# Three small moves in a retention and mixture-of-experts kernel: one subtraction to GpSimd, one copy to ScalarE, and the order of the loads

## The chip, the core and the metric

The kernel runs on one core of a Trainium2 chip. A core has five engines that run beside each other and wait for each other through semaphores: TensorE (PE in the profile, its weight loads PEld) multiplies matrices, VectorE (DVE) and ScalarE (ACT) do elementwise work, GpSimd (POOL) does elementwise work on on-chip memory and indirect transfers, and SyncE (SP) hands transfers to the core's DMA engines. Each engine works through its instructions in a fixed order. The metric is the device time of one execution in microseconds, lower is better.

## What is computed

The reference has two stages. The first is a retention layer for 8 sequences of 576 positions with 8 heads of width 64; the second sends each of the 4608 resulting rows to one of eight experts:

```
scores = q @ k^T / sqrt(64)                    # per head
ret    = scores * gamma[h] ** (i - j)  for i >= j, else 0
x      = ret @ v                               # 4608 rows of 512
expert = argmax(normalised x . normalised expert_emb / tau)
gate   = softmax(...)[expert]
out    = gate * (relu(x @ w1[expert]) @ w2[expert])    # w1 512x1024, w2 1024x512
```

All tensors are float32.

## The kernel before

**Retention.** A loop over the eight sequences (called batches, b = 0 to 7) holds a loop over four pairs of heads (p = 0 to 3). A sequence is cut into four chunks of 128 positions and a rest of 64. Within a chunk the masked scores are made directly: `emit_A` multiplies keys and queries on TensorE into a PSUM bank of the pool "a", and VectorE multiplies them by the triangle (line 623) into a buffer named raw. `emit_At` and line 719 do the same for the rest of 64 (tile pt). What earlier chunks contribute goes through a running state T: `emit_U(b)` multiplies keys and scaled values of each chunk into two PSUM banks of the pool "m" (rows named m<-vt,kt), and VectorE copies the first chunk's product into the state (line 651) and adds the others, one after the other (three instructions of line 653). `emit_QT` multiplies queries by the state and `emit_O` the scores by the values, both into a bank of the pool "o", of which there are two; `emit_Ot` does both for the rest of 64. `emit_X` (lines 705, 707 and 708) scales a finished "o" bank into the tile xT or xC on VectorE, and so frees the bank. The state of batch b+1 is made at the end of batch b.

**Loads.** `load_qk(b, p)` brings 576 KB of queries and keys of a pair of heads, `load_k(b)` 1024 KB of keys by chunk and `load_v(b)` 1152 KB of values, all for the next batch and all through SP (lines 481, 489 and 498). There are seven buffers for the first, two for each of the others. `scale_v(b)` multiplies the values by powers of gamma on GpSimd, in four instructions of 128x512 and one of 128x256 (lines 591 and 595); `emit_U(b)` needs them.

**Routing beside it.** Tasks of the batch before are set between the products: `route_tile` turns a 128-row tile of x by TensorE, ScalarE copies it from a PSUM bank to a buffer y (line 768), SP stores it to HBM (line 770, xd<-y), and ScalarE squares it (line 772). `route_head`, `route_rank`, `route_onehot` and `route_table` choose the experts on VectorE with small instructions (lines 207 to 341; line 209 subtracts the maximum, both of its inputs in on-chip memory).

**The first expert's weight.** In batches 2 to 5, at p = 1, one of the four tasks of `wsplit_tasks(0)` is started: SP loads a quarter of w1[0] (line 179, raw<-w, 512 KB), ScalarE rounds it to the high part (line 182), and VectorE subtracts that from the weight to get the low part (line 183). The experts' products use a high and a low part of weights and rows. Weights of n = 1 to 15 are split in the expert stage by the same function.

**Experts.** From about 180 us on TensorE runs the expert products (lines 120 and 971).

**What sets the order.** The program's text gives each instruction a priority by its place. A planner then goes through simulated time and hands each engine the first instruction by priority that it takes to be ready then. A load that the text has late can so come ahead of others when its buffer is free early (keys do so), and a store whose data is late falls behind. The resulting order of each engine is fixed, and on the chip an instruction that waits holds back all behind it on its engine.

Of the kernel before, what the change touches and what calls it, by code (L numbers as in the profile page):

```python
# [20 lines left out]
NP = H // 2  # L21
# [76 lines left out]
def retention_moe(ctx: ExitStack, tc: tile.TileContext, qk, kv, embT, tau, w1, w2, cst, out):  # L98
    nc = tc.nc
# [19 lines left out]
    def mm(*args, **kw):  # L119
        pe[:] = [nc.tensor.matmul(*args, **kw)]  # L120
        return pe[0]
# [5 lines left out]
    def behind():  # L127

        return ExitStack()
# [6 lines left out]
    def cc(name):  # L136
        o, w = _C[name]
        return cs[:, o : o + w]
# [27 lines left out]
    def wsplit_tasks(n):  # L166

        e, second = divmod(n, 2)
        src = (w2 if second else w1)[e]

        def step(c):
            raw = rawp.tile([P, RW], F32, name="raw")[:, :1024]
            if second:
                nc.sync.dma_start(
                    out=raw.rearrange("p (c n) -> p c n", c=2),
                    in_=src[c * 256 : (c + 1) * 256, :].rearrange("(c p) n -> p c n", p=P),
                )
            else:
                nc.sync.dma_start(out=raw, in_=src[c * P : (c + 1) * P, :])
            sl = wslot[n % 3]  # L180
            hi = sl[:, 0, c * 1024 : (c + 1) * 1024]
            nc.scalar.copy(hi, raw)  # L182
            nc.vector.tensor_tensor(  # L183
                out=sl[:, 1, c * 1024 : (c + 1) * 1024], in0=raw, in1=hi.bitcast(F32), op=ALU.subtract
            )

        return [lambda c=c: step(c) for c in range(4)]
# [283 lines left out]
    with ExitStack() as att:  # L471
# [7 lines left out]
        def load_qk(b, p):  # L479
            t = qkp.tile([P, 2, S], F32, name="qkt")  # L480
            nc.sync.dma_start(out=t, in_=qk[b, p])
            qkt[b, p] = t
# [4 lines left out]
        def load_k(b):  # L487
            t = a1.tile([P, KW], F32, name="kt", bufs=2)
            nc.sync.dma_start(out=t, in_=kv[b, :, :KW])
            kt[b] = t  # L490

        def load_v(b, split=False):
            t = a2.tile([P, KW + NP * D], F32, name="vt")
            if split:
                for lo, hi in [(c * DM, (c + 1) * DM) for c in range(NCH)] + [(KW, KW + NP * D)]:
                    nc.sync.dma_start(out=t[:, lo:hi], in_=kv[b, :, KW + lo : KW + hi])
            else:
                nc.sync.dma_start(out=t, in_=kv[b, :, KW:])
            vt_[b] = t
# [77 lines left out]
        def kview(b):  # L577
            return kt[b].rearrange("p (c n) -> p c n", c=NCH)

        def vview(b):  # L580
            return vt_[b][:, :KW].rearrange("p (c h d) -> p c h d", c=NCH, h=H)

        def vtview(b):
            return vt_[b][:, KW:].rearrange("p (r d) -> p r d", r=NP)

        def scale_v(b):
            eng = nc.vector if b == 0 else nc.gpsimd
            g = cc("gneg").rearrange("p (c h) -> p c h", c=NCH)
            v = vview(b)
            for c in range(NCH):  # L590
                eng.tensor_tensor(  # L591
                    out=v[:, c], in0=v[:, c], in1=g[:, c].unsqueeze(2).broadcast_to([P, H, D]), op=ALU.mult
                )
            vt = vtview(b)
            eng.tensor_tensor(
                out=vt, in0=vt, in1=cc("gnegt").unsqueeze(2).broadcast_to([P, NP, D]), op=ALU.mult
            )

        def turn_k(p):

            ps = psm.tile([P, 512], F32, name="m")
            for c in range(NCH):
                tr(ps[:, c * P : (c + 1) * P], qkt[0, p][:, 1, c * P : (c + 1) * P], ident)
            nc.scalar.copy(kview(0)[:, :, p * P : (p + 1) * P], ps.rearrange("p (c n) -> p c n", c=NCH))
# [3 lines left out]
        def emit_A(b, p):  # L608
            t = qkt[b, p]
            ps = [psa.tile([P, 512], F32, name="a") for _ in range(2)]  # L610
            for c in range(NCH):
                for h in range(2):
                    hs = slice(h * D, (h + 1) * D)
                    mm(
                        ps[h][:, c * P : (c + 1) * P],
                        t[hs, 1, c * P : (c + 1) * P],
                        t[hs, 0, c * P : (c + 1) * P],
                        start=True,
                        stop=True,
                    )  # L620
            pm = rawp.tile([P, RW], F32, name="raw")[:, :1024].rearrange("p (h c n) -> p h c n", h=2, c=NCH)
            for h in range(2):
                nc.vector.tensor_tensor(  # L623
                    out=pm[:, h],
                    in0=ps[h].rearrange("p (c n) -> p c n", c=NCH),
                    in1=tri.unsqueeze(1).broadcast_to([P, NCH, P]),
                    op=ALU.mult,
                )
            Pm[b, p] = pm

        def emit_U(b):
            k, v, T = kview(b), vview(b), Tst[b % 2]
            for c2 in range(NCH // 2):
                ps = psm.tile([P, 512], F32, name="m")
                u = ps.rearrange("p (c r d) -> p c r d", c=2, r=NP)
                for ci in range(2):
                    c = 2 * c2 + ci
                    for p in range(NP):
                        for h in range(2):
                            hd = 2 * p + h  # L640
                            mm(
                                u[h * D : (h + 1) * D, ci, p, :],
                                k[:, c, hd * D : (hd + 1) * D],
                                v[:, c, hd, :],
                                start=True,
                                stop=True,
                            )
                for ci in range(2):
                    c = 2 * c2 + ci
                    if c == 0:  # L650
                        nc.vector.tensor_copy(T[:, 0], u[:, 0])
                    else:
                        nc.vector.tensor_tensor(out=T[:, c], in0=u[:, ci], in1=T[:, c - 1], op=ALU.add)

# [178 lines left out]
        for b in range(B):  # L833
            for p in range(NP):
                if b + 1 < B:
                    load_qk(b + 1, p)
                    if p == 0:
                        load_v(b + 1)
                        load_k(b + 1)
                        scale_v(b + 1)  # L840
                if p + 1 < NP:
                    if b > 0 or p == 2:
                        with behind() if b > 0 else ExitStack():
                            emit_A(b, p + 1)
                else:
                    with behind():
                        if b + 1 < B:
                            emit_A(b + 1, 0)
                    with behind():
                        emit_At(b)  # L850
                    with behind():
                        if b + 1 < B:
                            emit_U(b + 1)
                if b == 0 and p == 0:
                    for r in range(NP):
                        turn_k(r)
                    emit_U(0)
                for _ in range(POPS[p] if b == B - 1 else 0):
                    if tasks:
                        tasks.pop(0)()  # L860
                if b == 0 and p < 2:
                    emit_O(b, p, True)
                    if p == 1:
                        emit_QT(b, 0, False)
                        emit_X(b, 0)
                        emit_X(b, 1)
                else:
                    if p % 2 == 0:
                        with behind():
                            emit_QT(b, p, True)  # L870
                    with behind() if b > 0 else ExitStack():
                        emit_O(b, p, False)
                    emit_X(b, p)
                if p == NP - 1:
                    with behind():
                        emit_Ot(b)
                if b < B - 1 and p in SLOTS and tasks:
                    with behind():
                        for task in tasks.pop(0):
                            task()  # L880
                if 1 < b < 6 and p == 1 and wq:
                    wq.pop(0)()
            if b < B - 1:
                tasks += route_tasks(b)
        b = B - 1
# [14 lines left out]
    with ExitStack() as moe:  # L900
# [88 lines left out]
        for e in range(NE):  # L989
            if e + 1 < NE:  # L990
                wq += wsplit_tasks(2 * e + 2)
            if e == 0:
                b = B - 1
# [241 lines left out]
```

## Time and profile before

| | |
|---|---|
| median of 3 runs | 612.83 us (610.84 to 613.12) |
| the profiled execution's own time | 612.28 us |
| its span, first to last instruction | 610.5 us |
| granted TensorE clock | 0.997 |
| PE busy, share of the span | 589.7 us, 97% |
| DVE, ACT, POOL busy | 330.7, 210.7, 176.8 us |
| bytes moved by DMA | 109.77 MB |

A row of a timeline reads: start in us from the span's start, length in us, engine, line, operation, output tile and input tiles, shape, how many instructions are merged in the row, and in brackets how long the engine was idle before it and what ended that. "SPq" is SyncE handing in a transfer. A row of grouped lines has the count, then busy time in us and mean ns of one, then the idle time before them with its causes. A row of waits has the total in us, the number of waits and the longest.

### The profile page before, as it was taken

How to read it: one execution, taken by the hardware profiler on the slowest of the kernel's cores; microseconds unless marked ns; L12 is line 12 of the kernel's file. 1: busy time of each engine (PE TensorE's matmuls, PEld its weight loads, DVE VectorE, ACT ScalarE, POOL GpSimd, SP SyncE). 2: the span in 40 equal slices, each digit the busy share in tenths (PEclk: the TensorE clock that was granted, in tenths of full speed). 3: DMA queues.
4: the chain of work that ended last, by engine and by line, in shares of the span. 5: the costliest groups of instructions: out<-in, count | busy, mean ns of one | idle time of the engine just before them, and what ended most of it. 6: DMA issues, size and time to landing. Idle time of an engine off the chain costs nothing. (4 is left out here: it accounts for less than half of the span.)

```text
span 610.5 us, 12786 instructions
## 1 busy us (share of the span) xinstructions
PE 589.7 (97%) x5249; PEld 521.8 (85%) x5249; DVE 330.7 (54%) x694; ACT 210.7 (35%) x397; POOL 176.8 (29%) x165
## 2 busy tenths in 40 slices
PE   9999989999999999999999999999999999999994
PEld 8877777777788888989988998898899889889974
DVE  5667785778768486671474067167337506632100
ACT  1032424242363445243434154244334414332111
POOL 1532033113236564304502250440450224020012
PEclk9999999999999999999999999999999999999998
DMA  8889888974356498773277166547627625610001
GB/s 307 296 352 326 314 288 310 339 281 164 112 193 202 144 206 298 137 220 124 78 188 238 61 141 191 181 129 159 213 71 171 238 77 132 147 51 30 2 18 63
DMA packets 73297, 109.77 MB, mean 180 GB/s; under 512 B 44634, under 2 KB 45054, under 8 KB 71424
## 3 DMA queue, kind: packets, MB, share of 16 engines
q1 hardware_dynamic: 65536, 88.63, 46.6%
q0 software_dynamic: 7680, 19.95, 10.2%
q8 instruction: 64, 1.05, 0.7%
q14 instruction: 17, 0.14, 0.1%
HBM read 79.96 MB, written 19.94 MB: 164 GB/s over the span
## 5 line engine op out<-in xcount | busy, mean ns | idle before, releaser
L971 PE MATMUL o<-wslot,hs 128*128 128x512 f32 (+1 forms) x816 | 186.6, 384 | 0.5 <-ACT y L978 0.4
L971 PEld LDWEIGHTS o<-wslot,hs 128*128 128x128 f32 x816 | 148.6, 188 | 29.5 <-ACT y L978 0.8
L120 PE MATMUL a<-xs,wslot 128*128 128x256 f32 (+1 forms) x864 | 116.1, 290 | 1.1 <-ACT xs L391 0.7
L120 PEld LDWEIGHTS a<-xs,wslot 128*128 128x128 f32 x864 | 112.2, 191 | 3.3 <-ACT xs L391 1.2
L979 POOL DMA_INDIRECT out<-y,sid x40 | 43.2, 1081 | 234.6 <-ACT y L978 191.6
L120 PE MATMUL m<-xs,wslot 128*128 128x320 f32 (+4 forms) x672 | 106.5, 314 | 0.4 <-issue 0.4
L120 PEld LDWEIGHTS m<-xs,wslot 128*128 128x128 f32 x672 | 102.5, 188 | 2.0 <-issue 0.9
L911 DVE SCALAR_TENSOR_TENSOR hs<-a,hs 128x256 fp32r<-128x256 f32 (+1 forms) x72 | 31.2, 436 | 124.0 <-ACT hs L910 105.0
L183 DVE TENSOR_TENSOR wslot<-raw,wslot 128x1024 fp32r<-128x1024 f32 x64 | 77.9, 1222 | 37.2 <-ACT wslot L182 35.7
L182 ACT CAST wslot<-raw 128x1024 fp32r<-128x1024 f32 x64 | 66.3, 1047 | 10.6 <-DMA raw<-w 10.0
L910 ACT ACTIVATE hs<-a 128x256 fp32r<-128x256 f32 (+1 forms) x72 | 28.3, 398 | 104.6 <-PE a L120 91.7
L369 POOL DMA_INDIRECT raw<-xd,gid x40 | 43.4, 1086 | 66.3 <-DVE wslot L183 24.5
L978 ACT ACTIVATE y<-o,gt 128x512 f32<-128x512 f32 (+1 forms) x34 | 22.6, 675 | 106.3 <-PE o L971 92.3
L591 POOL TENSOR_TENSOR vt<-vt,cs 128x512 f32<-128x512 f32 x28 | 28.3, 1043 | 90.9 <-DMA vt<-kv 74.2
L120 PE MATMUL a<-qkt 64*128 64x128 f32 (+1 forms) x640 | 47.8, 276 | 2.5 <-DVE raw L623 2.1
L380 POOL DMA_INDIRECT gt<-gd,gid x40 | 45.2, 1130 | 12.2 <-issue 11.9
L911 DVE SCALAR_TENSOR_TENSOR hs<-m,hs 128x384 fp32r<-128x384 f32 x56 | 30.7, 552 | 29.7 <-ACT hs L910 25.9
L120 PEld LDWEIGHTS a<-qkt 64*128 64x128 f32 (+1 forms) x640 | 39.2, 178 | 8.5 <-DVE raw L623 3.5
L623 DVE TENSOR_TENSOR raw<-a,tri 128x512 f32<-128x512 f32 x64 | 41.4, 684 | 5.5 <-PE a L120 5.5
L120 PE MATMUL o<-raw,vt 128*64 128x128 f32 x512 | 35.7, 278 | 0.0
L910 ACT ACTIVATE hs<-m 128x384 fp32r<-128x384 f32 x56 | 27.0, 492 | 21.7 <-PE m L120 18.1
L971 PE MATMUL m<-wslot,hs 128*128 128x512 f32 x144 | 33.6, 389 | 0.0
(141 smaller groups left out, 524.4 us busy)
## 6 DMA issues: line engine op xcount, KB each, us to landing
raw<-w SPq DMA_DIRECT2D x64, 512.0 KB
qkt<-qk SPq DMA_DIRECT2D x32, 576.0 KB
xd<-y SPq DMA_DIRECT2D x36, 256.0 KB
vt<-kv SPq DMA_DIRECT2D x7, 1152.0 KB
kt<-kv SPq DMA_DIRECT2D x7, 1024.0 KB
vt<-kv SPq DMA_DIRECT2D x4, 256.0 KB
raw<-xd,gid POOLq DMA_INDIRECT x40
gt<-gd,gid POOLq DMA_INDIRECT x40
```

What stands on the lines that cost most here:

```text
L120: pe[:] = [nc.tensor.matmul(*args, **kw)]
L182: nc.scalar.copy(hi, raw)
L183: nc.vector.tensor_tensor(out=sl[:, 1, c * 1024 : (c + 1) * 1024], in0=raw, in1=hi.bitcast(F32), op=ALU.subtract)
L369: return nc.gpsimd.indirect_dma_start(out=t[:, :DM], out_offset=None, in_=xd[:rows, :], in_offset=bass.IndirectOffsetOnAxis(ap=gid[:, a : ...
L380: nc.gpsimd.indirect_dma_start(out=g[:, i : i + 1], out_offset=None, in_=gd[:, :], in_offset=bass.IndirectOffsetOnAxis(ap=gid[:, a : a + 1 ...
L591: eng.tensor_tensor(out=v[:, c], in0=v[:, c], in1=g[:, c].unsqueeze(2).broadcast_to([P, H, D]), op=ALU.mult)
L623: nc.vector.tensor_tensor(out=pm[:, h], in0=ps[h].rearrange("p (c n) -> p c n", c=NCH), in1=tri.unsqueeze(1).broadcast_to([P, NCH, P]), op ...
L910: a = nc.scalar.activation(hi, ps[:, :n], AF.Relu)
L911: v = nc.vector.scalar_tensor_tensor(out=hs[:, 1, f, o : o + n], in0=ps[:, :n], scalar=0.0, in1=hi.bitcast(F32), op0=ALU.max, op1=ALU.subt ...
L971: nc.tensor.matmul(ps[:, :step], hs[:, hsp, f, i * P : (i + 1) * P], w[:, ws, f, n : n + step], start=(f == 0 and k == 0), stop=(f == NF - ...
L978: nc.scalar.activation(y[:, n : n + step], ps[:, :step], AF.Copy, scale=gts[e][:, i : i + 1])
L979: nc.gpsimd.indirect_dma_start(out=out[:, :], out_offset=bass.IndirectOffsetOnAxis(ap=sid[:, a : a + 1], axis=0), in_=y, in_offset=None, b ...
```

## The change

The subtraction that makes the low part of a weight runs on GpSimd when the weight is the first expert's w1 (n = 0), and on VectorE as before for the others. The copy that begins a state, 128x256 from PSUM, runs on ScalarE in place of VectorE. And the text orders the next batch's loads otherwise: at p = 0 it has the first two loads of queries and keys, the values, the keys by chunk, and the third load of queries and keys, and at p = 3 the fourth; before, it had one load of queries and keys at each p, and values and keys behind the first. The stores and the weight's load are traced in between as before.

```diff
@@ wsplit_tasks @@
             nc.scalar.copy(hi, raw)
-            nc.vector.tensor_tensor(
+            eng = nc.vector if n else nc.gpsimd
+            eng.tensor_tensor(
                 out=sl[:, 1, c * 1024 : (c + 1) * 1024], in0=raw, in1=hi.bitcast(F32), op=ALU.subtract
             )
@@ emit_U @@
                     if c == 0:
-                        nc.vector.tensor_copy(T[:, 0], u[:, 0])
+                        nc.scalar.copy(T[:, 0], u[:, 0])
                     else:
@@ the loop over batches and pairs @@
                 if b + 1 < B:
-                    load_qk(b + 1, p)
                     if p == 0:
+                        load_qk(b + 1, 0)
+                        load_qk(b + 1, 1)
                         load_v(b + 1)
                         load_k(b + 1)
+                        load_qk(b + 1, 2)
                         scale_v(b + 1)
+                    if p == NP - 1:
+                        load_qk(b + 1, 3)
```

## The prediction

> **What bounds the kernel now.** I read the page first, then the busy time in three stretches, then the waits of TensorE alone. The page's first rows:
>
> ```profile
> PE 589.7 (97%) x5249; PEld 521.8 (85%) x5249; DVE 330.7 (54%) x694; ACT 210.7 (35%) x397; POOL 176.8 (29%) x165
> ```
>
> TensorE is busy 589.7 of 610.5 us, so all its idle time is 20.8 us. The busy time by stretch (PE, PEld, DVE, ACT, POOL, then clock, DMA share, GB/s) says where it lies:
>
> ```profile
> 46.00:149.00 103.00, 96.31 (x1703) 79.21 (x1703) 76.70 (x208) 35.03 (x81) 23.09 (x25) 1.00 0.80 294
> 180.00:600.00 420.00, 417.91 (x2451) 379.27 (x2451) 203.32 (x339) 152.51 (x264) 131.50 (x116) 1.00 0.51 143
> ```
>
> From 180 us on TensorE idles 2.1 us in 420, and nothing of the change is there. In 46 to 149 us, five batches of the retention, it idles 6.7 us in 103, with the DMA engines at 0.80 and 294 GB/s. So this stage is close to a second bound, the transfers. The waits of TensorE in 46 to 149 us (total, count, longest), and GpSimd's longest:
>
> ```profile
> PE o L120 <- DVE xT L708: 2.3, 3, 0.9
> PE a L120 <- DVE raw L623: 1.8, 5, 0.4
> PE o L120 <- DVE xT L705: 1.2, 2, 0.7
> PE m L120 <- DVE pt L719: 0.9, 2, 0.6
> POOL vt L591 <- DMA vt<-kv: 73.8, 5, 17.5
> ```
>
> VectorE ends 2.3 + 1.8 + 1.2 + 0.9 = 6.2 us of them. That is the ceiling of what relief of VectorE can bring in these batches: 1%. No row has TensorE waiting for a load of queries and keys, so an earlier one has no wait of its own to remove. In order of time, the single waits at the ends of batches 1 to 5:
>
> ```profile
> 49.91 1.18 PE L120 MATMUL o<-qkt,Tst 64*64 64x128 f32 x24 [0.86 <-DVE xT L708]
> 69.79 0.95 PE L120 MATMUL o<-qkt,Tst 64*64 64x128 f32 x16 [0.44 <-DVE xT L705]
> 87.71 0.27 PE L120 MATMUL m<-pt,vt 64*64 64x64 f32 x2 [0.57 <-DVE pt L719]
> 90.12 1.07 PE L120 MATMUL o<-qkt,Tst 64*64 64x128 f32 x22 [0.73 <-DVE xT L708]
> 111.07 1.16 PE L120 MATMUL o<-qkt,Tst 64*64 64x128 f32 x22 [0.72 <-DVE xT L705]
> 130.97 1.18 PE L120 MATMUL o<-qkt,Tst 64*64 64x128 f32 x24 [0.73 <-DVE xT L708]
> ```
>
> `emit_QT` of the next batch waits for an "o" bank that VectorE frees last in a chain of its own: scores of the next batch, pt, the state's copy and three additions, then the bank.
>
> **The state's copy to ScalarE.** The grouped rows (busy, mean ns, idle before) give the durations of this and of the next part:
>
> ```profile
> L651 DVE COPY Tst<-m 128x256 f32<-128x256 f32 x8 | 3.3, 417 | 1.3 <-PE m L120 1.3
> L787 ACT COPY lt<-m 128x512 f32<-128x512 f32 x8 | 4.7, 586 | 58.3 <-PE m L120 58.3
> L787 ACT COPY lt<-m 128x128 f32<-128x128 f32 x4 | 1.1, 270 | 0.0
> L183 DVE TENSOR_TENSOR wslot<-raw,wslot 128x1024 fp32r<-128x1024 f32 x4 | 4.9, 1221 | 3.4 <-ACT wslot L182 3.4
> L591 POOL TENSOR_TENSOR vt<-vt,cs 128x512 f32<-128x512 f32 x28 | 28.3, 1043 | 90.9 <-DMA vt<-kv 74.2 <-DMA xd<-y 16.7
> ```
>
> It takes 0.42 us out of VectorE's chain, eight times. On ScalarE a copy from PSUM of 128x256 lies between the rows for 128x128 (0.27) and 128x512 (0.59): 0.38 us, the point between. ScalarE can begin when two of the four chunks are multiplied, while VectorE is still at scores, so I take it as hidden; the cover is gone if ScalarE is held (first rival). At 49.91 the wait falls from 0.86 to 0.44, a gain of 0.42.
>
> **The low part to GpSimd.** VectorE loses four subtractions of 1.22 us, and the 3.4 us for which it stood before them until ScalarE had rounded a weight that landed late. In batch 4 it looks so:
>
> ```profile
> 104.15 1.04 ACT L182 CAST wslot<-raw 128x1024 fp32r<-128x1024 f32 x1 [1.69 <-DMA raw<-w]
> 105.22 1.22 DVE L183 TENSOR_TENSOR wslot<-raw,wslot 128x1024 fp32r<-128x1024 f32 x1 [1.88 <-ACT wslot L182]
> 106.37 0.19 DVE L209 TENSOR_TENSOR L_all<-L_all,mx 128x40 f32<-128x40 f32 x1
> ```
>
> 3.1 us stand ahead of the routing and the next scores there. With the copy at least 1.22 + 0.42 = 1.64 us leave the chain in each of batches 2 to 5, more than any of their waits, so these go wholly: 0.44 + 0.57 + 0.73 + 0.72 + 0.73 = 3.19 us. The waits for line 623 come earlier in a batch and stay. On GpSimd the subtraction costs two times the 128x512 row, 2.1 us, and it follows `scale_v`; the five waits of 73.8 us hide it, and its result is first read at the end of the retention. Without that cover the next values would be 2.1 us late. Both edits: 0.42 + 3.19 = 3.6 us.
>
> It has a counter-force. VectorE's subtraction of the maximum takes 0.19 us above, but while GpSimd scales values it reads:
>
> ```profile
> 79.64 4.04 POOL L591 TENSOR_TENSOR vt<-vt,cs 128x512 f32<-128x512 f32 x4 [17.45 <-DMA vt<-kv]
> 82.69 1.04 DVE L209 TENSOR_TENSOR L_all<-L_all,mx 128x32 f32<-128x32 f32 x1
> 83.90 2.08 PE L120 MATMUL m<-vt,kt 128*64 128x64 f32 x64
> ```
>
> It ended at 83.73, just after GpSimd's fourth instruction at 83.68. So a longer GpSimd instruction can hold VectorE longer: anything from 0 to 2.1 us a batch. I take 0, since with the subtraction gone VectorE reaches these small instructions while GpSimd still waits for ScalarE; the upper end is the third rival. The Trainium skill's "SBUF — State Buffer" (section on who interferes with whom) says this outright: a VectorE instruction with two on-chip inputs and a GpSimd instruction that reads on-chip memory share a port pair, the first holds it for its whole length, and the other fully blocks. The trace agrees (1.04 against 0.19); by it alone, with every low part in the way, the two edits would be worth little more than the copy, 2.1 us in place of 3.6.
>
> **The loads.** SyncE's order at the start of batch 3, before, a load's size from the page, and two of the waits that bear on it:
>
> ```profile
> 66.79 0.33 SPq L489 DMA_DIRECT2D kt<-kv  x1
> 67.93 0.82 SPq L481 DMA_DIRECT2D qkt<-qk  x2
> 68.85 0.54 SPq L498 DMA_DIRECT2D vt<-kv  x1
> 74.31 0.81 SPq L770 DMA_DIRECT2D xd<-y  x2
> 75.17 0.43 SPq L481 DMA_DIRECT2D qkt<-qk  x1
> 75.70 1.66 SPq L179 DMA_DIRECT2D raw<-w  x1
> 77.80 0.33 SPq L481 DMA_DIRECT2D qkt<-qk  x1
> ```
> ```profile
> qkt<-qk SPq DMA_DIRECT2D x32, 576.0 KB
> ```
> ```profile
> 44.25 0.69 PE L120 MATMUL m<-vt,kt 128*64 128x64 f32 x16 [0.24 <-POOL vt L591]
> 45.25 0.69 PE L120 MATMUL m<-vt,kt 128*64 128x64 f32 x16 [0.32 <-POOL vt L591]
> ```
>
> The new text puts the load of 75.17 ahead of the values (68.85) and that of 77.80 ahead of the stores and the weight (74.31 to 75.70). Bytes stay the same. At 294 GB/s one load of 576 KB (0.59 MB) is 2.0 us, so the values land up to 2.0 us later, the weight up to 2.0 us, the stores up to 4.0 us. The stores have until a y buffer is needed again, three tiles on: 0 for them. In the batch that waited longest for its values (17.45 us idle, row of 79.64) GpSimd ended the fourth chunk at 83.68, and TensorE took it up at three quarters of 83.90 to 85.98, at 85.46: 1.8 us to spare, 0.2 us lost. The other late batches waited less, so I take 0 for them. But in batch 1 TensorE already waits twice for the values (44.25, 45.25), and a delay passes through whole: 2.0 us. Its bounds are 0, if the planner sets other products ahead of the state, and 2.0; I take 2.0, because the row nearest is this state itself, which waits. The late weight I take at 0, between 0 and the first rival's price.
>
> **Sum.** 612.28 (the profiled execution) − 3.6 + 2.0 + 0.2 = 610.9; the median of the runs stands 0.55 above the profiled execution, so 611.4 us.
>
> **Rivals.**
>
> First, slower: the weight 2.0 us late, with ScalarE's rounding at the head of its queue. Behind it stand the tile's copy and now the state's. In batch 4 the second half of the state already waits for that copy:
>
> ```profile
> 105.72 0.56 ACT L768 COPY y<-m 128x512 f32<-128x512 f32 x1
> 106.43 1.15 PE L120 MATMUL m<-vt,kt 128*64 128x64 f32 x32 [0.35 <-ACT y L768]
> ```
>
> There TensorE loses 2.0 less the 0.72 it need not wait later, 1.3 us; batch 2 has the same order of tiles, I put 1.0 on it (half the delay); batches 3 and 5 keep 0.57 + 0.2 + 0.2 of their gain, since the state's copy stands behind the rounding too, batch 1 its 0.42. In all −1.4 + 2.3 + 2.2 = +3.1: 615.9 us. For it: the wait of 1.69 us for the weight in the row of 104.15. Against: the planner may hand in the tile's copy first once it sees the weight later. It decides once the rounding stays ahead of that copy.
>
> Second: the planner sets batch 1's products so that the late values hurt nowhere, or leaves the loads about where they were. Then −3.6: 609.2 us. For it: TensorE has other products at a batch's end. Against: it did not do so at 44.25.
>
> Third: GpSimd's 2.1 us hold VectorE as long as its own subtraction did. Then only five copies count, −2.1 + 2.2: 612.9 us. For it the row of 82.69; against, the time at which the low parts come.
>
> **How the numbers follow.** Forecast 0.40, second rival 0.27, first 0.19, third 0.14. This kernel's measurement tells about 0.5%, 3.06 us, from no change: faster is under 609.77, slower over 615.89. The forecast gives 0.06 to faster (part of the waits for line 623, 1.8 us, may go too) and 0.02 to slower; the second rival 0.20 to faster, the first 0.10 to slower, the third 0.01 to each. That makes 0.27, 0.60 and 0.13. The forecast's own range is 609.4 (without its 2.0 us of loss) to 613.2 (half the gain lost). With the rivals: 608.0, the second with two thirds of the 1.8 us, to 616.0, the first.
>
> **What would show it.** No row of line 183 on VectorE before 150 us, and four GpSimd rows of about 2.1 us there; the state's copy on ScalarE at about 0.4 us, begun before pt is made; waits of 0.2 us or less before o<-qkt,Tst in batches 2 to 5; three loads of queries and keys and the values handed in ahead of two stores; GpSimd's values of batch 2 begun about 2 us later, and TensorE waiting 2 us more at 43 to 47 us. I am wrong if the span of 46 to 149 us keeps its idle time, if ScalarE's wait for the weight grows and is passed on, or if TensorE's own order is another.

## The result and the profile after

| | before | changed |
|---|---|---|
| median | 613.22 us (610.84 to 613.36, 6 runs) | 620.33 us (618.82 to 625.58, 6 runs) |
| ratio | | 1.0134, 95% interval 1.0093 to 1.0175 |
| span of the profiled execution | 610.5 us | 618.8 us |
| first product of the experts (a<-xs) begins at | 171.56 us | 174.58 us |
| first second-layer product of the second expert begins at | 249.46 us | 258.79 us |

The change made the kernel 1.3% slower. I forecast 611.4 us in a range of 608.0 to 616.0, so the result lies outside, on the other side of no change. The last two rows of the table divide the 8.3 us of span: 3.0 us are lost in the retention, 6.3 us between its end and the second expert, and 1.0 us of that is won back behind it. The two rows on which this rests in the changed kernel, from its timeline:

```profile
174.58 0.62 PE L120 MATMUL a<-xs,wslot 128*128 128x384 f32 x2
258.79 0.63 PE L976 MATMUL o<-wslot,hs 128*128 128x512 f32 x2
```

The line numbers of the changed kernel stand one higher than before from line 184 on, and five higher behind the loop over batches. The waits of TensorE, of the whole span (total, count, longest):

```profile
PE m L124 <- ACT y L769: 4.7, 3, 2.3
PE m L120 <- POOL vt L592: 2.9, 2, 1.8
PE a L120 <- DVE raw L624: 2.6, 6, 0.8
PE a L120 <- ACT xs L392: 1.6, 1, 1.6
...
PE m L120 <- ACT xs L392: 1.1, 1, 1.1
...
PE o L120 <- DVE xT L706: 0.3, 1, 0.3
...
PE o L120 <- DVE xT L709: 0.2, 1, 0.2
```

The waits for a bank (L706 and L709, 3.5 us before as L705 and L708) are nearly gone, as forecast. In their place stand 4.7 us for the copy of a tile on ScalarE, which no row of before had above 0.4 us, and 2.9 us for the values, 0.6 before. In order of time:

```profile
45.38 0.92 PE L120 MATMUL m<-vt,kt 128*64 128x64 f32 x14 [1.77 <-POOL vt L592]
66.32 0.33 PE L124 MATMUL m<-ident,lt 128*128 128x128 f32 x1 [2.26 <-ACT y L769]
88.23 0.98 PE L120 MATMUL m<-vt,kt 128*64 128x64 f32 x26 [1.10 <-POOL vt L592]
107.51 0.33 PE L124 MATMUL m<-ident,lt 128*128 128x128 f32 x1 [1.98 <-ACT y L769]
```

The second and the fourth lie in the even batches 2 and 4, in which the last three tiles of an odd batch are copied. What ScalarE waited for there, and what SyncE had handed in ahead, of batch 2:

```profile
62.76 0.59 ACT L769 COPY y<-m 128x512 f32<-128x512 f32 x1 [4.67 <-PE m L124]
65.68 0.58 ACT L769 COPY y<-m 128x512 f32<-128x512 f32 x1 [2.33 <-DMA xd<-y]
```
```profile
50.48 1.42 SPq L482 DMA_DIRECT2D qkt<-qk  x3
52.01 0.39 SPq L499 DMA_DIRECT2D vt<-kv  x1
52.44 0.43 SPq L482 DMA_DIRECT2D qkt<-qk  x1
56.18 0.89 SPq L771 DMA_DIRECT2D xd<-y  x2
```

The second tile's copy needs the y buffer whose store was handed in at 56.18, behind four loads of queries and keys and the values. ScalarE was ready for that buffer 7.2 us after the store was handed in, at 63.35; the copy begins 9.5 us after it, when the store has landed. Until then the tile holds its PSUM bank, and TensorE's next transposes wait for a bank.

### The profile page after: what moved, and what is told of

It reads as the page before. It is cut to its first block, busy times and chain, and to the rows that moved or that the text cites. A ratio compares the mean times of both kernels' runs of the same rounds, so it can differ in the third digit from the quotient of the medians.

```text
span 618.8 us, 12810 instructions
## 1 busy us (share of the span) xinstructions
PE 592.0 (96%) x5249; PEld 525.1 (85%) x5249; DVE 324.1 (52%) x682; ACT 213.9 (35%) x405; POOL 185.4 (30%) x169
## 5 line engine op out<-in xcount | busy, mean ns | idle before, releaser
L120 PEld LDWEIGHTS a<-xs,wslot 128*128 128x128 f32 x864 | 113.7, 193 | 3.7 <-ACT xs L392 1.9
L120 PE MATMUL m<-xs,wslot 128*128 128x320 f32 (+4 forms) x672 | 108.3, 317 | 1.9 <-ACT xs L392 1.1
L120 PEld LDWEIGHTS m<-xs,wslot 128*128 128x128 f32 x672 | 104.0, 190 | 3.9 <-ACT xs L392 1.5
L184 DVE TENSOR_TENSOR wslot<-raw,wslot 128x1024 fp32r<-128x1024 f32 x60 | 72.9, 1221 | 35.4 <-ACT wslot L182 35.2
L592 POOL TENSOR_TENSOR vt<-vt,cs 128x512 f32<-128x512 f32 x28 | 28.3, 1042 | 84.2 <-DMA vt<-kv 42.3
L769 ACT COPY y<-m 128x512 f32<-128x512 f32 x34 | 19.4, 585 | 45.5 <-PE m L124 32.5
```

Source lines behind the costliest of these rows:

```text
L184: eng.tensor_tensor(out=sl[:, 1, c * 1024 : (c + 1) * 1024], in0=raw, in1=hi.bitcast(F32), op=ALU.subtract)
L592: eng.tensor_tensor(out=v[:, c], in0=v[:, c], in1=g[:, c].unsqueeze(2).broadcast_to([P, H, D]), op=ALU.mult)
```

## The experiments

Theory A: the new order of loads costs, through two queues behind them, the values and the stores. Rival B: one of the two moved instructions costs. Two more theories came with what the profile after showed between 230 and 250 us.

### The loads alone and the moves alone

The loads alone are the changed kernel with

```diff
-            eng = nc.vector if n else nc.gpsimd
-            eng.tensor_tensor(
+            nc.vector.tensor_tensor(
...
-                        nc.scalar.copy(T[:, 0], u[:, 0])
+                        nc.vector.tensor_copy(T[:, 0], u[:, 0])
```

> The kernel before with the new order of the loads alone; both moved instructions stay on VectorE. Theory A (the loads ahead of the stores make values and y buffers late): the expert products begin about 4 to 6 us later than before, since the 3.0 us of the changed kernel hold a gain of 2 to 3 us from the moves, TensorE waits for the y copies 4 us or more and for the values about 3 us, and the time is 620 to 626 us. Rival B (the moves to GpSimd and ScalarE are what costs): within 2 us of before, 612 to 615 us.

Measured: 620.82 us, ratio 1.0107 (1.0040 to 1.0173); the experts begin at 177.48 us, 5.9 us late. TensorE waits 3.3 us for the values, as expected, and 1.9 us for the y copy, less than the 4 us expected. Beside the waits its granted clock is 0.97 in 46 to 149 us, against 1.00 before, which takes some 3 us more.

The moves alone are the changed kernel with the loop's loads as before.

> The kernel before with both moved instructions, the loads in their old order. Theory A: the waits of TensorE for VectorE at the batches' ends go, the expert products begin 2.5 to 3.6 us earlier, 609 to 611 us. Rival B: ScalarE's copy stands behind other work and GpSimd holds VectorE, the expert products begin later, 615 us or more.

Measured: 610.37 us, ratio 0.9945 (0.9918 to 0.9972); the experts begin at 167.85 us, 3.7 us early. TensorE's waits between 46 and 149 us:

```profile
PE a L120 <- DVE raw L624: 1.8, 5, 0.4
PE m L120 <- DVE pt L720: 1.7, 2, 1.4
PE o L120 <- DVE xT L709: 0.8, 2, 0.4
PE o L120 <- DVE xT L706: 0.3, 1, 0.3
```

Of the 3.5 us for banks 1.1 are left, but the waits for pt are 1.7 us and were 0.9. What VectorE ends in these batches so falls from 6.2 to 4.6 us, by 1.6 and not by the 3.6 of the sum. The rest of the 3.7 us has no wait of its own in these rows; two profiles of before differ by 1.6 us at that place. Rival B falls: what was lost came with the loads, and the moves by themselves gain.

### Each move alone

> The kernel before with the low part on GpSimd alone. By the prediction's terms 1.22 us leave VectorE's chain in batches 2 to 5, which is more than each wait there: the expert products begin about 3.2 us earlier than before's 171.6, so at 168.4, and the time is about 610 us. By the port rival (GpSimd holds VectorE for 2.1 us): no gain, 613 us.

Measured: 611.19 us, ratio 0.9954 (0.9920 to 0.9987), the experts from 168.07 us.

> The kernel before with the state's first copy on ScalarE alone. By the prediction's terms 0.42 us leave the chain in five batches: the expert products begin about 2.1 us earlier, at 169.5, and the time is about 611 us. If the copy on ScalarE comes later than VectorE's did (the three additions waited 3.3 us for it with both moves): no gain or slower, 613 to 614 us.

Measured: 611.44 us, ratio 0.9947 (0.9917 to 0.9977), the experts from 168.56 us. Each move gains by itself, and the two together (0.9945) gain no more than one that these runs can tell. Both shorten the same chain, so their gains can overlap; that this is the whole reason is not shown.

The third rival came true in a part of the batches. In the profile of the moves alone, GpSimd's subtraction, VectorE's comparison at line 216 (both of its inputs on-chip) and the wait that follows in batch 3:

```profile
82.78 2.38 POOL L184 TENSOR_TENSOR wslot<-raw,wslot 128x1024 fp32r<-128x1024 f32 x1 [0.29 <-ACT wslot L182]
82.80 2.41 DVE L216 TENSOR_TENSOR oh<-wm,wme 128x32 bf16<-128x32 f32 x1
87.03 0.27 PE L120 MATMUL m<-pt,vt 64*64 64x64 f32 x2 [1.44 <-DVE pt L720]
```

The comparison of batch 2 took 0.20 us; this one ended just after GpSimd, and TensorE's wait for pt, 0.57 us before, became 1.44. The same instruction took 2.03 us in batch 4 of this profile and 2.34 us in batch 2 of the subtraction alone. Of the eight low parts in the two profiles three so held VectorE for 2 us or more; in the profile of the changed kernel none did. The net of the move was still a gain.

### Four y buffers, and the values first

If the y buffers are what the stores hold up, one more should free ScalarE, with every engine's order but a few of ScalarE's own as it was:

```diff
-    my = ctx.enter_context(tc.tile_pool(name="my", bufs=3))
+    my = ctx.enter_context(tc.tile_pool(name="my", bufs=4))
```

> The changed kernel with four y buffers in place of three, so that a tile's copy need not wait until the store of the third tile before it has landed; the orders of TensorE and of the transfers are the same. Theory A: ScalarE's 13.0 us of waits for the stores and TensorE's 4.7 us for the y copies fall under 1 us each, the waits for the values (2.9 us) stay, the expert products begin 3 to 4.5 us earlier than in the changed kernel, and the time is 613 to 617 us. If the stores are not the cause: 619 to 621 us.

Measured: 617.24 us, ratio 1.0059 (1.0026 to 1.0092). The rows of ScalarE's copies up to 180 us, first of the changed kernel, then with four buffers:

```profile
L769 ACT COPY y<-m 128x512 f32<-128x512 f32 x34 | 19.4, 585 | 45.5 <-PE m L124 32.5 <-DMA xd<-y 13.0
```
```profile
L769 ACT COPY y<-m 128x512 f32<-128x512 f32 x34 | 18.9, 587 | 34.5 <-PE m L124 32.4 <-DMA xd<-y 2.0
```

ScalarE's 13.0 us for stores fall to 2.0 (under 1 was expected), TensorE's wait for the copies is gone, and the experts begin at 171.45 us. Of the 2.9 us for the values 2.0 are left. The median lies just above the expected 613 to 617 us.

The other half, the values and the keys by chunk traced ahead of the second load of queries and keys:

```diff
                         load_qk(b + 1, 0)
-                        load_qk(b + 1, 1)
                         load_v(b + 1)
                         load_k(b + 1)
+                        load_qk(b + 1, 1)
                         load_qk(b + 1, 2)
```

> The changed kernel with the values and the keys by chunk traced ahead of the second load of queries and keys; all three loads still stand ahead of the stores. Theory A: TensorE's waits for the values (2.9 us) fall to about 0.6 us as before, those for the y copies (4.7 us) stay, the expert products begin about 1.5 to 2.5 us earlier than in the changed kernel; 617 to 620 us. If the late values are the larger part: 613 to 615 us.

Measured: 617.36 us, ratio 1.0072 (1.0044 to 1.0101). TensorE's waits up to 200 us:

```profile
PE m L124 <- ACT y L769: 4.3, 3, 2.5
PE a L120 <- DVE raw L624: 2.6, 6, 0.8
PE m L120 <- POOL vt L596: 1.1, 1, 1.1
...
PE m L120 <- POOL vt L592: 0.6, 2, 0.3
```

The waits for the values fall from 2.9 to 1.7 us, those for the y copies stay. The experts begin at 171.35 us, earlier than expected, and the median is as expected.

### Both mended

> The changed kernel with the values and keys by chunk ahead of the second load of queries and keys, and with four y buffers. Theory A: both kinds of waits go (values under 1 us, y copies under 1 us), the expert products begin as early as with the two moves alone, 167 to 169 us, and the time is 609 to 613 us. If something else in the new order of loads costs: expert products from 170.5 us on, 614 us or more.

Measured: 609.54 us, ratio 0.9940 (0.9910 to 0.9970). The experts begin at 167.23 us, and between 46 and 149 us no wait for values or y copies is left:

```profile
PE o L120 <- DVE xT L709: 2.2, 3, 1.6
PE a L120 <- DVE raw L624: 1.8, 5, 0.4
PE m L120 <- DVE pt L720: 0.6, 1, 0.6
PE m L124 <- ACT lt L788: 0.2, 1, 0.2
```

With both waits away the kernel is where the moves alone put it, and faster than either kernel of this study's start, so no cost of the new order is left that the runs can tell. The 1.6 us in the first row are the first rival's wait as it was written: ScalarE's rounding waited for the weight, the state's copy stood behind it, and the bank came late.

```profile
84.98 1.04 ACT L182 CAST wslot<-raw 128x1024 fp32r<-128x1024 f32 x1 [2.93 <-DMA raw<-w]
86.33 1.41 DVE L654 TENSOR_TENSOR Tst<-m,Tst 128x256 f32<-128x256 f32 x3 [1.33 <-ACT Tst L652]
```

To see whether the fourth buffer by itself gives anything:

> The two moves with the loads in their old order, and four y buffers; the orders of all engines are as with the moves alone. There ScalarE waited 0.6 us for a store in all, so theory A expects no change against the moves alone: within 1 us of 610.4. Should the y buffers bound something that the waits do not show, it is 2 us or more faster.

Measured: 610.47 us, ratio 0.9958 (0.9926 to 0.9989), the experts from 167.47 us. It gives nothing where stores do not queue behind loads, and the loads handed in early give nothing that can be told from their old order (0.9940 against 0.9958, and 0.9945 for the moves with three buffers).

### Where the second expert begins

The changed kernel lost more behind the retention than in it. From its profile, 230 to 250 us (PE, PEld, DVE, ACT, POOL, clock, DMA share, GB/s), and the same stretch of before:

```profile
230.00:250.00 20.00, 16.25 (x82) 14.62 (x81) 12.59 (x19) 9.79 (x17) 7.52 (x6) 0.83 0.90 250
```
```profile
230.00:250.00 20.00, 18.98 (x137) 18.36 (x136) 12.78 (x19) 11.10 (x19) 11.22 (x11) 1.00 0.70 251
```

TensorE idles 3.75 us there against 1.0 before, and its granted clock is 0.83 in the mean. In steps of half a microsecond it reads 0.50 from 237.0 to 240.0 and from 244.0 to 246.5 us; 0.17 of 20 us are 3.4 us of full clock lost, or 6.8 us at half. With the 2.75 us of further waits that makes 6.2 us, of the 6.3 that this part took longer. To keep TensorE busy in those waits, small products were set into them:

```diff
+            if e == 1 and fs[0] == 0:
+                for _ in range(24):
+                    mm(wide[0][:, :P], ones, ones, start=True, stop=True)
             pick(width, 0, len(WIDTHS), body)
...
-                pb = mm1_in(e, f, 1)
+                pb = psa.tile([P, 512], F32, name="a")
+                if e == 1 and f == 0:
+                    for _ in range(28):
+                        mm(pb[:, :P], ones, ones, start=True, stop=True)
+                mm1_in(e, f, 1, pb)
```

> The changed kernel with two groups of small matrix products that nothing uses, 24 and 28 of 128x128, set ahead of the second expert's first products, where TensorE waited for that expert's rows (3.8 us of waits at 234 to 244 us, and there the granted clock fell to half for two stretches of 3.4 us). Theory C (short waits make the clock fall, and the half clock costs as much as the waits): the clock stays at full there, the products take no more than the waits, and the time falls by about 3 us, to 616 to 618.5 us. Rival D (the clock falls for another reason, or the wait alone matters): the same or up to 2 us slower, 620 to 623 us.

Measured: 616.19 us, ratio 1.0045 (1.0007 to 1.0083), against 620.08 for the changed kernel in the same comparison. The two halves of the stretch:

```profile
230.00:240.00 10.00, 10.00 (x67) 8.69 (x66) 7.85 (x12) 5.17 (x8) 2.24 (x1) 1.00 1.04 258
240.00:250.00 10.00, 10.00 (x92) 9.87 (x91) 6.86 (x11) 6.56 (x11) 5.53 (x6) 1.00 0.80 291
```

The clock is at full where the waits are filled, as theory C expected, and a kernel with added work that computes nothing was 3.9 us faster. How much of the 3.9 us the clock gave is not shown, because the planner also gave the filled kernel another order of later products. From the second expert's first product into an "m" bank (m<-wslot,hs, at 278.63 us, in the changed kernel at 280.63) to the end its profile takes 336.1 us, and all 13 others take 338.2 to 340.3: 2.1 us or more of the gain lie where nothing was filled in. What stands without this run is the sum above: in this stretch the new waits cost about twice their length.

### The same kernels again

> The changed kernel once more, beside the others. The expert products begin within 1 us of 174.6 us, and the waits for the y copies (4 to 5 us) and for the values (2.5 to 3.5 us) are there again. If what was lost where the second expert begins (from 174.6 to 258.8 us, 84.2 us, 6.3 more than before) belongs to the change, it is 82 us or more again; if it is chance, it lies anywhere from 78 to 85 us.

Measured: 620.08 us, ratio 1.0093 (1.0050 to 1.0136). Its profile is of its longest execution, 626 us, in which the retention ended at 182.2 us, so not within 1 us of 174.6; the waits for the y copies (4.9 us) and the values (3.7 us) are there again. Its granted clock in 46 to 149 us is 0.92, against 0.99 in the first profile, some 7 us of full clock, about as much as it came later. From the first expert product to the second expert it took 80.7 us.

> The kernel before once more, for a second profile: the expert products begin within 1 us of 171.6 us. From there to the second expert's products it took 77.9 us in the first profile; if that is chance it lies anywhere from 78 to 83 us now, with or without a stretch of half clock.

Measured: 612.92 us, ratio 0.9983 (0.9946 to 1.0020) to itself, which says what this measurement can tell; the experts from 170.00 us, 1.6 us earlier than in the first profile, and 78.8 us to the second expert.

> The changed kernel with four y buffers once more: its runs lay between 613.4 and 619.5 us while its profile was of one of the fastest. If the spread comes from stretches of half clock that follow the wait for the values in batch 1, a profile of a slower run has two or more such stretches in the retention or where the second expert begins; if it comes from that place alone, the retention ends within 0.5 us of 171.5 us again. Median 615 to 618 us.

Measured: 616.26 us, ratio 1.0031 (0.9991 to 1.0070). The experts begin at 172.76 us and need 82.6 us to the second expert, where TensorE waits 2.6 us for ScalarE; this profile has a stretch at less than full clock in each of the two places, at 48 and at 240 us. The faster profile of the same kernel had the one at 48 us too (0.91 in 40 to 60 us in both), but none at 240. Of the 4.9 us between the two spans 3.3 lie at the second expert and 1.3 in the retention, and the 1.3 are not explained by the clock.

That part took 77.9 to 81.8 us in the six profiles with the loads in their old order (77.9, 78.8, 79.9, 79.6, 81.3, 81.8) and 79.3 to 84.2 in the seven others (84.2, 80.7, 82.2, 79.3, 82.6, 82.5, 82.0), leaving out the filled one (79.4), whose order of products is another. The 84.2 us of the first profile were in good part chance; whether the new order of loads makes that part longer by itself stays open.

## Why the prediction was wrong

**What bounds the kernel: right.** 97% of TensorE, a retention near its transfers, 6.2 us as the ceiling. That a second resource was near its end should have weighed more: a new order of transfers has no spare time to take its delays from.

**The state's copy: right.** I put ScalarE's copy between 0.27 and 0.59 us at 0.38; the third row below has 370 ns. Rows of the changed kernel up to 180 us:

```profile
L184 POOL TENSOR_TENSOR wslot<-raw,wslot 128x1024 fp32r<-128x1024 f32 x4 | 9.5, 2378 | 2.5 <-ACT wslot L182 2.5
L654 DVE TENSOR_TENSOR Tst<-m,Tst 128x256 f32<-128x256 f32 x24 | 10.1, 423 | 6.7 <-ACT Tst L652 4.6 <-PE m L120 1.0
L652 ACT COPY Tst<-m 128x256 f32<-128x256 f32 x8 | 3.0, 370 | 8.2 <-PE m L120 8.2
L182 ACT CAST wslot<-raw 128x1024 fp32r<-128x1024 f32 x4 | 4.1, 1035 | 0.0
```

It was less well hidden than I said: the additions wait 4.6 us for it in these eight batches, where VectorE's own copy took 3.3 us. Alone it still gained 0.5%, between 1.4 and 5.1 us, which takes in the 2.1 us of its terms.

**The low part: a gain, but not by the sum.** It took 2.38 us on GpSimd, not 2.1. Both moves brought 0.9945 in the runs and the experts 3.7 us earlier in the profile, where the sum had 3.6. That they agree is in part luck: the waits that were to go wholly, 3.19 us in batches 2 to 5, did not (at 87.71 one grew from 0.57 to 1.44 us), and VectorE's rows fell by 1.6 us only. The counter-force was taken at 0 and was 2 us or more in three low parts of eight. That line 623's waits stay was right (1.8 us).

**The values: right in sum, off in both terms.** In batch 1 the wait is 1.77 us at 45.38, against 0.56 in two waits before, so 1.2 us more where I had 2.0. At 88.23 it is 1.10 us, and my term there was 0.2. Together 2.3 us more, and the forecast had 2.2.

**The stores: the step that failed.** "The stores have until a y buffer is needed again, three tiles on: 0 for them." I had worked out that they would land up to 4.0 us later and then priced that at nothing without a row for the time until a buffer is needed. In batch 2 the buffer was needed 7.2 us after its store was handed in, the store of 56.18 landed after 9.5 us, and the copy of 65.68 waited 2.33 us for it. 4.7 us of TensorE's waits hung on it, the largest term of the whole sum, and four buffers took it away. With it the forecast would have been 611.4 + 4.7 = 616.1 us, slower than before.

**The weight: its place was wrong, its form was right.** The first rival had ScalarE held at its queue's head, the tile's copy late, and TensorE without a bank. All of that came in the changed kernel, but there ScalarE was held by the store and not by the weight: its rounding waited 0.0 us for the weight up to 180 us (last row above). The rival's 615.9 us was nearest to the result.

**What no step had: the clock.** The sum took each wait at its length. At the second expert 2.75 us of new waits came with 3.4 us of lost clock, and in the retention of the changed kernel the clock also fell once, behind the 1.77 us at 45.38 (the stretch holds 0.09 below full, 3.6 us at half). The stretch, and a part of it:

```profile
40.00:60.00 20.00, 17.89 (x298) 14.84 (x292) 12.00 (x35) 6.18 (x15) 4.61 (x5) 0.91 0.77 289
46.00:48.50 2.50, 2.50 (x42) 2.20 (x41) 0.42 (x1) 1.62 (x4) 2.50 (x4) 0.50 0.31 116
```

The page's row of clocks could have told me to ask: before, it is at nine tenths or more in every slice but the last, so that any new wait could cost more than itself.

**Superposed.** Mending one wait gave about 3 us, mending both gave 10.5 (620.1 to 609.5). That either one of the remaining waits still drops the clock would explain it, and both profiles of four y buffers have such a stretch behind the values' wait; it is not shown that this is all of it.

## What to carry to other kernels

A load that is handed in ahead of a store takes the store's place, and what waits for the store is whoever needs its source buffer next: count the buffers, look up when the next one is needed, and put a row beside it before the delay is priced at nothing. Put the load first on which something waits (here the values) and the loads that nobody waits for last. Where TensorE runs at full clock, price a new wait at up to about twice its length, and make a change of several parts one at a time: here two parts together gained 0.5% and the third by itself lost 1.1%.

## What the runs showed of the hardware

Behind some waits of 1 to 2.9 us TensorE's granted clock was at half for some 3.4 us, and behind others it was not. The Trainium skill, "TensorE: Matmul & The Clock Gate" (Part 1), has the clock in two states, full and half, judged over free-running windows of about 3.4 us, and names an idle window of that length as what brings half. The first part agrees with the stretches here (0.91 and 0.83 of 20 us are one and two such windows at half); the second does not, since no wait ahead of these stretches reached 3.4 us: 1.77 us at 45.38 were followed by such a stretch, and the longest of these waits was 2.9 us (values first, for ScalarE's rows of the second expert). The length of a wait alone does not decide. In the changed kernel the clock stayed at 1.00 behind 2.26 us at 66.32 and 1.98 us at 107.51; in the filled kernel, whose retention is the same, it stayed at 1.00 behind 1.82 us at 45.80 and 2.81 us at 67.05, and fell behind 2.47 us at 108.68 (0.91 in 100 to 120 us). What else decides stays open.

A subtraction of 128x1024 float32 with both inputs in on-chip memory took 2378 ns on GpSimd and 1221 ns on VectorE, and while it ran on GpSimd a comparison on VectorE took 2.41 us in place of 0.2. A store of 256 KB handed in behind loads landed after 9.5 us.
